# Seven block products for the last layer of the second half of the tokens, and kept weight parts in DRAM

## The chip, the cores and the metric

The kernel runs on one core of one Trainium2 chip. The metric is device microseconds for one execution, as the median of three runs. A core has TensorE (matmuls, written PE in the profile, with its weight loads listed apart as PEld), VectorE (DVE), ScalarE (ACT), GpSimd (POOL) and SyncE (SP), which here only issues transfers. Each engine works through its own instructions in order and waits for other engines by semaphores. Matmul results land in PSUM, which the kernel uses as eight banks of 128 x 512 float32; its GpSimd instructions have all operands in SBUF.

## The reference

```python
x = A_u                                             # 1 x 2048 x 512
h = x + _A_ref(_layernorm(x), ...)                  # a long convolution over the tokens
h2 = h + _B_ref(_layernorm(h), w1, w2, w3, w4)

def _B_ref(x, w1, w2, w3, w4):
    h = _gelu(_layernorm(x) @ w1)                   # layer 1, then a shift of tokens
    hs = shifted(h) @ w2                            # layer 2
    x1 = x + hs
    h2 = _gelu(_layernorm(x1) @ w3) @ w4            # layer 3: 512 -> 1792, layer 4: 1792 -> 512
    return x1 + h2
```

The change is in layers 3 and 4 alone: 2048 tokens, hidden width 1792.

## The kernel before

**Precision.** Each factor of a product is held as a high part (float32r) and a low part (the rest), and a product is three matmuls: high x high, high x low, low x high (`PROD`). A high part is made by ScalarE (a cast, or the GELU written out as float32r), a low part by a subtraction, source minus high part, on VectorE or GpSimd. GELU is therefore done twice on ScalarE: once into the high part, once into a float32 tile from which the low part is taken.

**Layer 3 in seven products.** The loop at the end of `mixer_phase` has 14 steps, `s` = 0 to 13: seven for the first 1024 tokens, seven for the second (`half` is 7). A step makes two hidden blocks of 128, number f and f + 7, for two groups of 512 tokens. That is a 2 x 2 block product and is made from seven block products, a, b, c, e (in `layer3a`) and f, d, g (in `layer3b`), instead of eight: sums and differences of weight blocks (`s1` to `s4`, made by GpSimd in `sum3`) meet sums and differences of activations (`t1` to `t4`). A product is six matmuls (two chunks of 128 of the 512 inputs' halves, three part products) with 512 moving columns into one PSUM bank. VectorE adds the seven banks up (`plus`), ScalarE copies the first. `raw3` loads the weight blocks, `sum3` sums them, `load3` makes their high and low parts on ScalarE and GpSimd. The homes of the parts alternate between odd and even steps.

**Layer 4 before.** The hidden blocks are the stationary operand and the rows of `w4` the moving one: `layer4(s, q, i, ...)` makes 128 tokens of output from the two hidden blocks of the step, six matmuls of 512 columns. A step makes eight such groups, so 48 matmuls, one step after its layer 3: `layer4a(s - 1)` adds four groups up in four PSUM banks that are held over seven steps (`acc`), `layer4b(s - 1)` writes four groups to fresh banks that VectorE adds to `h` in SBUF. At the end of each half `h` gets the last addend and `store` sends it out, four transfers of 64 KB for each 128 tokens; for the second half two of the four are issued by ScalarE's queue. `raw4` and `load4` fetch `w4` and make its parts.

**What sets the order.** `InOrder` keeps the program's order on TensorE, VectorE, ScalarE and GpSimd; transfers are issued by SyncE unless said otherwise. PSUM has four rotating banks (`bank`) and the four that are held (`wide_bank`). A bank is used again when VectorE or ScalarE has read it. VectorE's instructions stand in the order: sums of layer 3 as the products come, low parts of the activations between them, then the additions to `h`.

Of the kernel before, what the change touches and what calls it, by code (L numbers as in the profile page):

```python
# [1150 lines left out]
def mixer_phase(ctx, tc, cst, h, out, finish, w3, w4):  # L1151

    nc = InOrder(tc)
    pool = lambda name, bufs, **kw: ctx.enter_context(tc.tile_pool(name=name, bufs=bufs, **kw))
    sl = pool("slab", 44)
    tm = pool("tm", 6)
    w1a, w1p = pool("wrap0", 1), pool("wrap", 1)
    sm = pool("sm", 2)
    ps = pool("ps2", 4, space=PSUM)
    pa = pool("pacc", 1, space=PSUM)  # L1160
    ident = cst["ident"]
# [2 lines left out]
    def slab(name):  # L1164
        return sl.tile([128, 512], F32R, tag="slab", name=name)

    def slot(i):
        return cst["slab"](i)

    def tmp(name):  # L1170
        return tm.tile([128, 512], F32, tag="g", name=name, bufs=5)

    XQ = [(w1p if i else w1a).tile([128, 4 * 512], F32, name=f"xq{i}") for i in range(4)]
    X1 = {0: XQ[3], 1: XQ[1], 2: XQ[2], 3: XQ[0]}
    quarter = lambda t, i: t[:, i * 512 : i * 512 + 512]
    turned = lambda t: t.rearrange("p (a c x) -> p c a x", a=4, c=4)
# [22 lines left out]
    PROD = ((0, 0), (0, 1), (1, 0))  # L1199
# [47 lines left out]
    def turn1(q):  # L1247
        XT[q] = transposed(XL.pop(q), f"xt{q}", 2 if q == 3 else 0)
# [71 lines left out]
    xq = {}  # L1320
# [79 lines left out]
    def some(n):  # L1400
        while n and todo:
            todo.pop(0)()
            n -= 1


    W3S = [w1p.tile([128, 512], F32R, name=f"w3s{i}") for i in range(2)]
    raw = {n: w1p.tile([128, k * 512], F32, name=f"raw{n}") for n, k in (("a", 1), ("b", 1), ("4", 1), ("5", 1), ("s", 2))}

    def raw3(s):
        f = s % half  # L1410
# [5 lines left out]
    def sum3():  # L1416
# [4 lines left out]
        nc.gpsimd.tensor_tensor(s2, s1, a11, ALU.subtract)  # L1421
        nc.gpsimd.tensor_tensor(s4, a12, s2, ALU.subtract)

    def load3(s, low=nc.gpsimd, parts=range(3)):
        ra, a22, sm_ = raw["a"], raw["b"][:, 256:512], raw["s"]
        if s % 2:
            one, four, last = (slot(11), slot(14)), (slots(4, 2), slots(6, 2)), slot(8)
        else:
            one, four, last = (slot(20), W3S[0]), (slots(16, 2), slots(18, 2)), W3S[1]
        for i, (src, (hi, lo)) in enumerate(((ra, one), (sm_, four), (a22, (last[:, 0:256], last[:, 256:512])))):  # L1430
            if i not in parts:
                continue
            nc.scalar.copy(hi, src)
            low.tensor_tensor(lo, src, hi.bitcast(F32), ALU.subtract)
        at_ = lambda w, i: w[:, i * 256 : i * 256 + 256]
        W3[s] = dict(a11=[at_(w, 0) for w in one], a12=[at_(w, 1) for w in one], a22=[at_(last, i) for i in range(2)],
                     **{f"s{i + 1}": [at_(w, i) for w in four] for i in range(4)})

    def raw4(s):
        for i in range(2):  # L1440
            f = s % half + i * half
# [48 lines left out]
    t1, t3, t2, t4 = ([S[c][i] for c in range(2)] for i in range(4))  # L1490
# [64 lines left out]
    def store(j):  # L1555
        for c in range(4):
            queue = nc.scalar if j >= 8 and c % 2 else nc.sync
            queue.dma_start(ov[c][:, j, :], h[c * 32 : c * 32 + 32, j, :])

    def layer4(s, q, i, b, first, last):  # L1560
        for k in range(2):
            for n, (wi, xi) in enumerate(PROD):
                nc.tensor.matmul(b, H3[s, k, q][xi][:, i * 128 : i * 128 + 128], W4[s][k][wi],
                                 start=(first and k == 0 and n == 0), stop=(last and k == 1 and n == 2))

    def layer4a(s):
        first, last = s % half == 0, s % half == half - 1
        for i in range(4):
            if first:
                acc[i] = wide_bank(i, f"acc{s}_{i}")  # L1570
            layer4(s, 0, i, acc[i], first, last)
            j = s // half * 8 + i
            if last:
                nc.vector.scalar_tensor_tensor(h[:, j, :], h[:, j, :], off1[:, j : j + 1], acc[i], ALU.add, ALU.add)
                store(j)

    def layer4b(s, late):
        for i in range(4):
# [14 lines left out]
            for c in range(2):  # L1593
                halve(FT[1, "sums", c][n], 1, n, c)

    for s in range(2 * half):
        turn, last = s + 1 == half, s + 1 == 2 * half
        layer3a(s)
        if turn:
            fresh(("b11", "t2", "t3", "t1"))  # L1600
        if last:
            load4(s)
        else:
            load3(s + 1, *((nc.gpsimd,) if s else (nc.vector, (2,))))
        if s + 2 < 2 * half:
            raw3(s + 2)
        if s:
            layer4a(s - 1)
        if s == 1:
            for j in range(8, 12):  # L1610
                residual(j), stats2(j)
        if s == 2:
            for j in range(12, 16):
                stats2(j)
            norm2(2)
            for j in range(12, 16):
                residual(j)
# [7 lines left out]
        if not last and s:  # L1625
            load4(s), raw4(s + 1)
        if s + 2 < 2 * half:
            sum3()
        if s:
            layer4b(s - 1, late)  # L1630
        else:
            late()
        some(4)
        if turn:
            fresh(("b21", "t4", "b22"))
    layer4a(2 * half - 1), layer4b(2 * half - 1, lambda: None)


@with_exitstack
# [41 lines left out]
```

## Time and profile before

| | |
|---|---|
| timed runs | 684.05, 684.76, 684.91 us; median 684.76 |
| profiled execution, first to last instruction (its span) | 683.0 us |
| busy over the span: PE, DVE, ACT, POOL | 640.8, 547.9, 415.5, 402.9 us |
| step 0 of the loop starts (first matmul of `l3a`) | 392.1 us |
| step 7 starts (second half) | 524.7 us |
| step 13 starts | 647.1 us |

The page gives no other time of the profiled execution than its span; the median of the runs lies 1.8 us above the span. In the rows of the profile every line is L86, since the wrapper of `InOrder` records each instruction; tiles tell them apart. `l3a` to `l3g` are the banks of layer 3, `acc` the held banks and `l` (or `l4`) the fresh banks of layer 4, `u` the float32 sums of layer 3, `h_...h` and `h_...l` high and low parts of activations. Names such as `cs0w`, `amp0w`, `sn1w` and `ptw` are buffers of the first part of the kernel that now hold weights. A row of the timeline has the start in us, the duration in us, engine, line, operation, output, inputs, shape and count; the bracket behind is the engine's idle time before it and what ended it.

### The profile page before, as it was taken

Reading aid. Unit: us, or ns where it says so; the run is one execution under the profiler, and the core shown is the slowest. Engines: PE = TensorE matmul, PEld = TensorE weight load, DVE = VectorE, ACT = ScalarE, POOL = GpSimd, SP = SyncE. Lnnn points to the kernel's source line nnn. Section 1 sums busy time; section 2 is a strip of 40 time slices with the busy share of each in tenths; the row PEclk is TensorE's granted clock in tenths of the full one; section 3 lists DMA queues with packets and bytes.
Section 4 is the critical chain, followed back from the end, with each engine's and each line's share of the span. In section 5 each row is a group of like instructions: output and inputs, shape, how many; then the busy total and the mean of one; then the engine's idle time right before and its main releaser. Section 6 shows DMA issues by size and latency. Waiting matters only on the chain.

```text
span 683.0 us, 17273 instructions
## 1 busy us (share of the span) xinstructions
PE 640.8 (94%) x7044; PEld 501.2 (73%) x7044; DVE 547.9 (80%) x935; ACT 415.5 (61%) x731; POOL 402.9 (59%) x421
## 2 busy tenths in 40 slices
PE   2985999899999999999999999999999999999997
PEld 2972755673577685768888878888888888888885
DVE  6989989999998999889978798866789954455554
ACT  6998978978889886246634454544375443354330
POOL 1878499878999998402676219355635555554210
PEclk9996999999999999999999999999999999999999
DMA  8840554011301133020232312133312342211004
GB/s 214 241 168 18 157 159 125 2 49 34 65 18 34 34 110 96 2 63 1 63 92 56 100 32 62 32 101 105 103 32 53 87 138 62 63 47 47 24 9 123
DMA packets 49267, 51.52 MB, mean 75 GB/s; under 512 B 6436, under 2 KB 33060, under 8 KB 49188
## 3 DMA queue, kind: packets, MB, share of 16 engines
q1 hardware_dynamic: 47524, 47.80, 24.7%
q10 hardware_dynamic: 1152, 1.57, 1.0%
q0 software_dynamic: 512, 1.05, 0.6%
q8 instruction: 55, 0.90, 0.6%
q14 instruction: 24, 0.20, 0.1%
HBM read 35.72 MB, written 8.39 MB: 65 GB/s over the span
## 4 chain that ended last, share of the span: by engine, by line
PE 67%; ACT 12%; DVE 11%; POOL 5%; issue 3%; DMA 0%; SPq 0%; ACTq 0%; POOLq 0%; DVEq 0%
PE l L86 24%; PE bank L86 12%; PE acc L86 11%; ACT pt L86 7%; DVE cs L86 3%; PE l3e L86 3%; PE l3b L86 3%; PE l3a L86 3%; PE l3g L86 3%; PE l3d L86 3%; PE l3f L86 3%; PE l3c L86 3%; DVE sn L86 2%; POOL pt L86 2%; DVE u L86 1%
## 5 line engine op out<-in xcount | busy, mean ns | idle before, releaser
L86 POOL TENSOR_TENSOR pt<-p,s 128x512 int32<-128x512 int32 x64 | 73.3, 1161 | 8.6 <-DVE sn L86 8.1
L86 ACT ACTIVATE pt<-pt 128x1056 f32<-128x1056 int32 x64 | 69.8, 1091 | 12.5 <-DVE cs L86 6.4
L86 PE MATMUL bank<-at,tbs 128*64 128x128 f32 (+1 forms) x768 | 63.1, 311 | 2.8 <-ACT u L86 0.9
L86 PEld LDWEIGHTS bank<-at,tbs 128*64 128x64 f32 x768 | 44.7, 134 | 19.1 <-ACT at L86 2.1
L86 PE MATMUL bank<-u,ms 64*128 64x128 f32 x736 | 47.5, 278 | 5.7 <-DVE u L86 1.9
L86 PEld LDWEIGHTS bank<-u,ms 64*128 64x128 f32 x736 | 43.1, 188 | 9.7 <-DVE u L86 2.6
L86 POOL TENSOR_TENSOR cs0w<-raw,cs0w 128x512 fp32r<-128x512 f32 x7 | 9.1, 1297 | 58.8 <-ACT cs0w L86 58.8
L86 PE MATMUL bank<-cs 128*32 128x64 f32 x1024 | 33.1, 228 | 11.0 <-ACT kt L86 5.7
L86 DVE TENSOR_TENSOR cs<-pt,amx 128x512 f32<-128x512 f32 x64 | 41.2, 680 | 2.3 <-ACT amx L86 1.7
L86 PEld LDWEIGHTS bank<-cs 128*32 128x32 f32 x1024 | 24.3, 113 | 24.2 <-POOL pt L86 8.4
L86 POOL TENSOR_TENSOR sn1w<-raw,sn1w 128x512 fp32r<-128x512 f32 x7 | 9.5, 1359 | 54.0 <-ACT sn1w L86 42.1
L86 DVE TENSOR_TENSOR h<-h,l 128x512 f32<-128x512 f32 x48 | 32.0, 685 | 10.6 <-PE l L86 10.6
L86 PE MATMUL bank<-ident 128*128 128x128 f32 x292 | 39.6, 293 | 0.0
L86 DVE TENSOR_TENSOR u<-u,l3f 128x512 f32<-128x512 f32 x14 | 9.5, 682 | 36.9 <-PE l3f L86 36.9
L86 ACT COPY at<-bank 128x512 f32<-128x512 f32 x44 | 26.9, 623 | 19.2 <-PE bank L86 19.2
L86 PEld LDWEIGHTS bank<-ident 128*128 128x128 f32 x292 | 36.5, 204 | 2.8 <-DVE at L86 1.1
L86 ACT ACTIVATE pt<-pt,halfpi 128x1056 f32<-128x1056 f32 x32 | 37.8, 1182 | 0.5
L86 ACT ACTIVATE u<-u 128x512 f32<-128x512 f32 x56 | 35.4, 632 | 1.8
L86 POOL TENSOR_TENSOR cs<-pt,amp 128x512 f32<-128x512 f32 x26 | 31.8, 1223 | 5.6 <-ACT pt L86 2.9
L86 DVE STREAM_TRANSPOSE at<-bank 128x512 f32<-128x512 f32 (+1 forms) x36 | 32.8, 950 | 1.4 <-PE bank L86 1.4
L86 PE MATMUL bank<-sn 128*32 128x64 f32 x1024 | 32.5, 225 | 0.0
L86 POOL TENSOR_TENSOR sn<-pt,amp 128x512 f32<-128x512 f32 x24 | 29.5, 1230 | 4.8 <-issue 3.7
(1180 smaller groups left out, 2112.8 us busy)
## 6 DMA issues: line engine op xcount, KB each, us to landing
raw<-in_B_w_dram SPq DMA_DIRECT2D x28, 256.0 KB, 2.7
xq<-xq SPq DMA_DIRECT2D x72, 64.0 KB, 2.0
h<-in_A_u_dram SPq DMA_DIRECT2D x32, 128.0 KB, 4.2
h<-in_A_u_dram SPq DMA_DIRECT2D x16, 256.0 KB, 3.9
rawa<-in_B_w_dram SPq DMA_DIRECT2D x14, 256.0 KB, 2.8
rawb<-in_B_w_dram SPq DMA_DIRECT2D x14, 256.0 KB, 2.9
ms<-in_mm_dram SPq DMA_DIRECT2D x4, 768.0 KB, 10.9
out_dram<-h SPq DMA_DIRECT2D x48, 64.0 KB, 1.7
```

Of the source, the lines that this page charges most:

```text
L86: ins = f(*args, **kw)
```

## The change

Three things change in the loop.

1. **Weight parts of layer 3 are kept.** In the first half each step's seven tiles of high and low parts of `w3` (256 KB each) are written to DRAM (`keep3`, five transfers from SyncE's queue). In the second half `fetch3` reads them back one step ahead, five transfers, in place of `raw3`, `sum3` and `load3`.
2. **Layer 4 of steps 7 to 12 is made from seven products.** The output for 1024 tokens is a 2 x 2 block product as well: two groups of 512 tokens by two halves of 256 output columns, with the two hidden blocks in the middle. `prod4` makes one product: 12 matmuls with 256 moving columns into two banks. VectorE makes sums of activations (`sum4`), ScalarE their high parts (`cast4`), VectorE their low parts (`low4`); GpSimd makes sums and low parts of the `w4` blocks (`load4s`). The products `a11 b11` and `s2 t2` are added up in the four held banks (`res`) over six steps. `v`, `w` and `z` are added to `h` by VectorE (`collect`); `x` and `y`, which two output blocks need, are added up in SBUF (`held`).
3. **Low parts of the second half's hidden blocks are made by GpSimd** instead of VectorE.

In step 13 the parts that were held back are brought into `h`: GpSimd adds `held` (eight additions), ScalarE copies two held banks to `both`, VectorE makes `total`, GpSimd adds both to two output blocks (four additions), `x` and `y` are collected twice each, and VectorE adds `total` to the two other blocks (four additions). Step 13's own layer 4 is done as before, 48 matmuls of 512 columns, behind the loop. Step 7 still does the old layer 4 for step 6.

```diff
+    def homes3(s):
+        if s % 2:
+            return (slot(11), slot(14)), (slots(4, 2), slots(6, 2)), slot(8)
+        return (slot(20), W3S[0]), (slots(16, 2), slots(18, 2)), W3S[1]
...
+    def keep3(s):
+        one, four, last = homes3(s)
+        for far, w in zip(kept[s], (*one, *four, last)):
+            nc.sync.dma_start(far, w.bitcast(F32))
+    def fetch3(s):
+        one, four, last = homes3(s)
+        for far, w in zip(kept[s - half], (*one, *four, last)):
+            nc.sync.dma_start(w.bitcast(F32), far)
+        names3(s)
...
-    for s in range(2 * half):
+    for s in range(half):
...
-        if last:
-            load4(s)
+        if turn:
+            fetch3(s + 1)
         else:
             load3(s + 1, *((nc.gpsimd,) if s else (nc.vector, (2,))))
...
+        if s == 0:
+            keep3(0)
         if turn:
             fresh(("b21", "t4", "b22"))
-    layer4a(2 * half - 1), layer4b(2 * half - 1, lambda: None)
+        else:
+            keep3(s + 1)
...
+    def load4s(s):
+        b1, b2, t = raw["4"], raw["5"], raw["s"]
+        t1, t2, t3, t4 = (part2(t, i) for i in range(4))
+        nc.gpsimd.tensor_tensor(t1, part2(b1, 1), part2(b1, 0), ALU.subtract)
...
+        for src, pair in ((part2(b1, 0), one), (b2, two), (t, four)):
+            nc.scalar.copy(pair[0], src)
+            low_of(pair, src, nc.gpsimd)
...
+    def prod4(s, x, w, banks, more=False, done=True):
+        for n, b in enumerate(banks):
+            for i in (2 * n, 2 * n + 1):
+                for k, (wi, xi) in enumerate(PROD):
+                    nc.tensor.matmul(part2(b, i % 2), OPS[s, x][xi][:, i * 128 : i * 128 + 128], B4[s][w][wi], ...)
...
+    for s in range(half, 2 * half):
+        last, pre = s + 1 == 2 * half, s - 1
+        summed = pre >= half
+        if not last:
+            fetch3(s + 1)
+        if last:
+            for k, c in ((0, (0, 1)), (1, (1, 0)), (0, (1, 1)), (1, (1, 1))):
+                for d, b in zip(columns(*c), held[k]):
+                    nc.gpsimd.tensor_tensor(d, d, b, ALU.add)
+        one = slab(f"one_{s}").bitcast(F32)
+        nc.scalar.copy(one, prod(s, "a", "a11", "b11"))
+        if summed:
+            sum4(pre, "s1", "a21", "a22", ALU.add)
+            sum4(pre, "s2", "s1", "a11", ALU.subtract)
+            sum4(pre, "s3", "a11", "a21", ALU.subtract, SRC[pre, "a21"])
+            for n in ("s2", "s1", "s3"):
+                cast4(pre, n)
+        two, three, four = (tmp(f"{n}_{s}") for n in ("two", "three", "four"))
+        plus(two, prod(s, "b", "s2", "t2"), one)
+        if summed:
+            sum4(pre, "s4", "a12", "s2", ALU.subtract)
+            cast4(pre, "s4")
+            low4(pre, "s2"), low4(pre, "s1")
+        plus(three, prod(s, "c", "s3", "t3"), two)
+        if summed:
+            low4(pre, "s3"), low4(pre, "s4")
+        b = prod(s, "e", "s1", "t1")
+        plus(four, b, three)
+        plus(two, b, two)
+        gelus3(s, "a22", four, four)
+        low4(s, "a22", nc.gpsimd)
+        plus(one, prod(s, "f", "a12", "b21"), one)
+        gelus3(s, "a11", one, one)
+        low4(s, "a11", nc.gpsimd)
+        if summed:
...
+            prod4(pre, "a11", "b11", res[:2], pre > half, last)
+            prod4(pre, "s2", "t2", res[2:], pre > half, last)
+        else:
+            layer4a(pre)
+        (load4 if last else load4s)(s)
+        if not last:
+            raw4(s + 1)
+        if last:
+            both, total = ([slab(f"{n}{i}").bitcast(F32) for i in range(2)] for n in ("both", "total"))
+            for i in range(2):
+                nc.scalar.copy(both[i], res[i])
+            for i in range(2):
+                nc.vector.tensor_tensor(total[i], res[2 + i], both[i], ALU.add)
+            for c, src in (((0, 0), both), ((1, 1), total)):
+                for d, b in zip(columns(*c), src):
+                    nc.gpsimd.tensor_tensor(d, d, two_tiles(b), ALU.add)
+        plus(three, prod(s, "d", "a22", "t4"), three)
+        gelus3(s, "a12", three, three)
+        plus(two, prod(s, "g", "s4", "b22"), two)
+        gelus3(s, "a21", two, two, last)
+        if not last:
+            low4(s, "a12", nc.gpsimd)
+        if not summed:
+            layer4b(pre, lambda: None)
+            continue
+        for n, x, w, c in (("v", "a12", "b21", (0, 0)), ("w", "s4", "b22", (0, 1)), ("z", "a22", "t4", (1, 0))):
+            b = fresh_banks(s, n)
+            prod4(pre, x, w, b)
+            collect(columns(*c), b)
+            if last and n == "w":
+                low4(s, "a12")
+        for k, n, x, w, c in ((0, "x", "s1", "t1", (0, 1)), (1, "y", "s3", "t3", (1, 0))):
+            b = fresh_banks(s, n)
+            prod4(pre, x, w, b)
+            if last:
+                collect(columns(*c), b), collect(columns(1, 1), b)
+            else:
+                collect(held[k], b, pre == half)
+        if last:
+            low4(s, "a21")
+            for c in ((0, 1), (1, 0)):
+                for d, b in zip(columns(*c), total):
+                    nc.vector.tensor_tensor(d, d, two_tiles(b), ALU.add)
...
+        for i in range(4):
+            b = bank(f"l4_{s}_{q}{i}") if q else wide_bank(i, f"acc{s}_{i}")
+            layer4(s, q, i, b, True, True)
+            j = 8 + 4 * q + i
+            nc.vector.scalar_tensor_tensor(h[:, j, :], h[:, j, :], off1[:, j : j + 1], b, ALU.add, ALU.add)
+            store(j)
```

More of the change, by code (lines that the diff above doesn't have):

```diff
@@ L1158, in mixer_phase @@
     sm = pool("sm", 2)
+    w3p = pool("kept", 1, space=bass.MemoryType.DRAM)
     ps = pool("ps2", 4, space=PSUM)
@@ L1171, in tmp @@
         return tm.tile([128, 512], F32, tag="g", name=name, bufs=5)
-    XQ = [(w1p if i else w1a).tile([128, 4 * 512], F32, name=f"xq{i}") for i in range(4)]
+    XQ = [(w1p if i else w1a).tile([128, 4 * 512], F32, tag=f"xq{i}", name=f"xq{i}") for i in range(4)]
     X1 = {0: XQ[3], 1: XQ[1], 2: XQ[2], 3: XQ[0]}
@@ L1406, in mixer_phase @@
     W3S = [w1p.tile([128, 512], F32R, name=f"w3s{i}") for i in range(2)]
-    raw = {n: w1p.tile([128, k * 512], F32, name=f"raw{n}") for n, k in (("a", 1), ("b", 1), ("4", 1), ("5", 1), ("s", 2))}
+    raw = {n: w1p.tile([128, k * 512], F32, tag=f"raw{n}", name=f"raw{n}") for n, k in (("a", 1), ("b", 1), ("4", 1), ("5", 1), ("s", 2))}
     def raw3(s):
@@ L1422, in sum3, with names3 @@
         nc.gpsimd.tensor_tensor(s4, a12, s2, ALU.subtract)
+    def homes3(s):
+        if s % 2:
+            return (slot(11), slot(14)), (slots(4, 2), slots(6, 2)), slot(8)
+        return (slot(20), W3S[0]), (slots(16, 2), slots(18, 2)), W3S[1]
+    def names3(s):
+        one, four, last = homes3(s)
+        at_ = lambda w, i: w[:, i * 256 : i * 256 + 256]
+        W3[s] = dict(a11=[at_(w, 0) for w in one], a12=[at_(w, 1) for w in one], a22=[at_(last, i) for i in range(2)],
+                     **{f"s{i + 1}": [at_(w, i) for w in four] for i in range(4)})
+    kept = {s: [w3p.tile([128, n * 512], F32, name=f"kept{s}{i}") for i, n in enumerate((1, 1, 2, 2, 1))] for s in range(half)}
+    def keep3(s):
[3 more added lines that the diff above has]
+    def fetch3(s):
+        one, four, last = homes3(s)
+        for far, w in zip(kept[s - half], (*one, *four, last)):
+            nc.sync.dma_start(w.bitcast(F32), far)
+        names3(s)
     def load3(s, low=nc.gpsimd, parts=range(3)):
         ra, a22, sm_ = raw["a"], raw["b"][:, 256:512], raw["s"]
[L1426 to L1429, printed above, removed]
+        one, four, last = homes3(s)
         for i, (src, (hi, lo)) in enumerate(((ra, one), (sm_, four), (a22, (last[:, 0:256], last[:, 256:512])))):
@@ L1434, in load3 @@
             low.tensor_tensor(lo, src, hi.bitcast(F32), ALU.subtract)
-        at_ = lambda w, i: w[:, i * 256 : i * 256 + 256]
-        W3[s] = dict(a11=[at_(w, 0) for w in one], a12=[at_(w, 1) for w in one], a22=[at_(last, i) for i in range(2)],
-                     **{f"s{i + 1}": [at_(w, i) for w in four] for i in range(4)})
+        names3(s)
     def raw4(s):
@@ L1594, in fresh @@
                 halve(FT[1, "sums", c][n], 1, n, c)
-    for s in range(2 * half):
-        turn, last = s + 1 == half, s + 1 == 2 * half
+    for s in range(half):
+        turn = s + 1 == half
         layer3a(s)
@@ L1600, in mixer_phase @@
             fresh(("b11", "t2", "t3", "t1"))
-        if last:
-            load4(s)
+        if turn:
+            fetch3(s + 1)
         else:
             load3(s + 1, *((nc.gpsimd,) if s else (nc.vector, (2,))))
-        if s + 2 < 2 * half:
+        if s + 2 < half:
             raw3(s + 2)
@@ L1624, in mixer_phase @@
         late = layer3b(s)
-        if not last and s:
+        if s:
             load4(s), raw4(s + 1)
-        if s + 2 < 2 * half:
+        if s + 2 < half:
             sum3()
@@ L1633, in mixer_phase @@
         some(4)
+        if s == 0:
+            keep3(0)
         if turn:
             fresh(("b21", "t4", "b22"))
-    layer4a(2 * half - 1), layer4b(2 * half - 1, lambda: None)
+        else:
+            keep3(s + 1)
+    XH = [(w1p if i else w1a).tile([128, 4 * 512], F32R, tag=f"xq{i}", name=f"xh{i}") for i in range(4)]
+    spare = w1p.tile([128, 512], F32R, tag="rawa", name="spare")
+    side = lambda i, k: (quarter(XH[i // 2], i % 2 * 2 + k))
+    SUM = {n: (side(i, 0), side(i, 1)) for i, n in enumerate(("s1", "s2", "s3", "s4"))}
@@ new lines, in mixer_phase, with low_of @@
+    part2 = lambda w, i: w[:, i * 256 : i * 256 + 256]
+    pairs = lambda i: XH[2].bitcast(F32).rearrange("p (n t d) -> p n t d", n=4, d=256)[:, i]
+    held = [[pairs(i), pairs(2 + i)] for i in range(2)]
+    OPS, B4, SRC = {}, {}, {}
+    def low_of(pair, src, eng=nc.vector):
+        eng.tensor_tensor(pair[1], src, pair[0].bitcast(F32), ALU.subtract)
+    def load4s(s):
+        b1, b2, t = raw["4"], raw["5"], raw["s"]
+        t1, t2, t3, t4 = (part2(t, i) for i in range(4))
+        nc.gpsimd.tensor_tensor(t1, part2(b1, 1), part2(b1, 0), ALU.subtract)
+        nc.gpsimd.tensor_tensor(t3, part2(b2, 1), part2(b1, 1), ALU.subtract)
+        nc.gpsimd.tensor_tensor(t2, part2(b2, 1), t1, ALU.subtract)
+        nc.gpsimd.tensor_tensor(t4, part2(b2, 0), t2, ALU.subtract)
+        if s % 2:
+            four, two, one = (slots(9, 2), slots(12, 2)), (quarter(XH[3], 3), slot(15)), spare
+        else:
+            four, two, one = (slots(0, 2), XH[3][:, 0:1024]), (slot(2), slot(3)), quarter(XH[3], 2)
+        one = part2(one, 0), part2(one, 1)
+        for src, pair in ((part2(b1, 0), one), (b2, two), (t, four)):
+            nc.scalar.copy(pair[0], src)
+            low_of(pair, src, nc.gpsimd)
+        B4[s] = dict(b11=one, b21=[part2(w, 0) for w in two], b22=[part2(w, 1) for w in two],
+                     **{f"t{i + 1}": [part2(w, i) for w in four] for i in range(4)})
@@ new lines, in prod4, with columns @@
+    def prod4(s, x, w, banks, more=False, done=True):
+        for n, b in enumerate(banks):
+            for i in (2 * n, 2 * n + 1):
+                for k, (wi, xi) in enumerate(PROD):
+                    nc.tensor.matmul(part2(b, i % 2), OPS[s, x][xi][:, i * 128 : i * 128 + 128], B4[s][w][wi],
+                                     start=(i % 2 == 0 and k == 0 and not more), stop=(i % 2 == 1 and k == 2 and done))
+    def columns(q, c):
+        return [h[:, 8 + 4 * q + 2 * n : 10 + 4 * q + 2 * n, c * 256 : c * 256 + 256] for n in range(2)]
@@ new lines, in mixer_phase, with collect, gelus3 @@
+    two_tiles = lambda b: b.rearrange("p (t d) -> p t d", t=2)
+    def collect(dst, banks, new=False):
+        for d, b in zip(dst, banks):
+            if new:
+                nc.vector.tensor_copy(d, two_tiles(b))
+            else:
+                nc.vector.tensor_tensor(d, two_tiles(b), d, ALU.add)
+    def gelus3(s, name, src, dst, high=True):
+        if high:
+            OPS[s, name] = slab(f"h_{name}{s}h"), slab(f"h_{name}{s}l")
+            nc.scalar.activation(OPS[s, name][0], src, AF.Gelu_apprx_tanh)
+        nc.scalar.activation(dst, src, AF.Gelu_apprx_tanh)
+        SRC[s, name] = dst
@@ new lines, in sum4 @@
+    def sum4(s, name, a, b, op, dst=None):
+        t = slab(f"{name}_{s}f").bitcast(F32) if dst is None else dst
+        nc.vector.tensor_tensor(t, SRC[s, a], SRC[s, b], op)
+        SRC[s, name], OPS[s, name] = t, SUM[name]
+    cast4 = lambda s, name: nc.scalar.copy(OPS[s, name][0], SRC[s, name])
+    low4 = lambda s, name, eng=nc.vector: low_of(OPS[s, name], SRC[s, name], eng)
+    fresh_banks = lambda s, name: [bank(f"l4{name}{n}_{s}") for n in range(2)]
+    res = None
+    for s in range(half, 2 * half):
[33 more added lines that the diff above has]
+        if summed:
+            if pre == half:
+                res = [wide_bank(i, f"res{i}") for i in range(4)]
+            prod4(pre, "a11", "b11", res[:2], pre > half, last)
+            prod4(pre, "s2", "t2", res[2:], pre > half, last)
+        else:
+            layer4a(pre)
[31 more added lines that the diff above has]
+                collect(columns(*c), b), collect(columns(1, 1), b)
+            else:
+                collect(held[k], b, pre == half)
[4 more added lines that the diff above has]
+                    nc.vector.tensor_tensor(d, d, two_tiles(b), ALU.add)
@@ L1639, in tile_kernel @@
+    s = 2 * half - 1
+    for q in range(2):
+        for k in range(2):
+            H3[s, k, q] = OPS[s, ("a11", "a12", "a21", "a22")[2 * q + k]]
+        for i in range(4):
[4 more added lines that the diff above has]
+            store(j)
 @with_exitstack
```

## The prediction

> **What bounds the kernel now.** I read the page first, then busy time by stage, then the chain of waits.
>
> ```profile
> span 683.0 us, 17273 instructions
> PE 640.8 (94%) x7044; PEld 501.2 (73%) x7044; DVE 547.9 (80%) x935; ACT 415.5 (61%) x731; POOL 402.9 (59%) x421
> ```
> ```profile
> core 0: us, PE busy (x) PEld busy (x) DVE busy (x) ACT busy (x) POOL busy (x), PEclk, DMA share, GB/s
> 606.30:626.70 20.40, 20.40 (x91) 16.90 (x90) 10.08 (x15) 8.55 (x14) 9.70 (x10) 1.00 0.17 52
> 647.13:683.00 35.87, 31.44 (x139) 25.72 (x137) 16.52 (x24) 6.79 (x11) 2.54 (x2) 0.99 0.27 72
> ```
> ```profile
> 626.89 1.36 PE l3a L86 x6
> ...
> 647.29 1.36 PE l3a L86 x6
> ...
> 673.13 5.45 PE l L86 x24
> ```
>
> TensorE is busy 94% of the span. The stage row 606.30:626.70 is one whole step of the second half (step 11): 20.40 us, TensorE busy in all of it at full clock, VectorE for 10.08, ScalarE 8.55, GpSimd 9.70. The chain holds matmuls alone, one step every 20.40 us (647.29 less 626.89), to the end at 678.58. So what leaves other engines in a step is worth nothing; only shorter TensorE work is, as long as no other engine takes the bound. Step 13 and what follows it last 35.87 us; I call that stage the tail.
>
> **Part one, the matmuls.**
>
> ```profile
> 569.84 0.39 PE L86 MATMUL l3e<-t110l,cs1w 128*128 128x512 f32 x1
> 570.06 0.39 PE L86 MATMUL l3e<-t110h,sn0w 128*128 128x512 f32 x1
> ...
> 258.61 1.61 PE L86 MATMUL bank<-ident 128*128 128x128 f32 x13
> ...
> 291.55 1.88 PE L86 MATMUL bank<-h,ident 128*128 128x512 f32 x4
> ```
> ```profile
> 258.62 1.42 PEld L86 LDWEIGHTS bank<-ident 128*128 128x128 f32 x12
> ```
> ```profile
> L86 PEld LDWEIGHTS acc<-cs0w,h_000h x8: 187/188/188, 407.1 to 412.0; 128*128 128x128 f32 x8
> ```
> ```profile
> L86 PE MATMUL bank<-ident x292: 275/275/422, 14.6 to 291.4; 128*128 128x128 f32 x146
> ...
> L86 PE MATMUL bank<-h,ident x20: 592/592/697, 156.3 to 295.8; 128*128 128x512 f32 x20
> ```
>
> A product of six matmuls takes 1.36, so a matmul of 512 columns comes every 0.2267 us. A step now has 42 for layer 3 (9.52) and 48 for layer 4 (10.88). In steps 8 to 13 the 48 become 7 x 12 = 84 matmuls of 256 columns, each with a weight load of its own. No row shows a float32r matmul of 256 columns. Bounds: the 13 `ident` matmuls, each with a load of 128 columns, take 1.61 us, the last of them 0.275 of it: (1.61 - 0.275) / 12 = 0.111 from one to the next, load included, and I take that as the least. From above: the recorded load, 0.188, if none of it is hidden. Between them lies half of 0.2267, 0.113, if all the time goes with the columns. I take 0.120: of the plain float32 kind, 128 columns cost 0.111 and 512 cost (1.88 - 0.59) / 3 = 0.43, so 0.00083 a column and 0.005 beside them; a float32r matmul of 512 in 0.2267 must run at about half that per column, 0.21, which leaves 0.0135 to 0.016 that don't go with the columns, and 256 then take 0.120 to 0.121. So 84 x 0.120 = 10.08, a gain of 0.80 a step; at 0.111 it is 1.56, at 0.188 a loss of 4.91. Five steps (8 to 12) earn 4.0 (7.8; -24.6); step 13 is treated below. Step 7 stays at 20.40.
>
> [...]
>
> **Part two, VectorE and GpSimd in steps 8 to 12.**
>
> ```profile
> 443.22 1.88 DVE L86 TENSOR_TENSOR h<-h,l 128x512 f32<-128x512 f32 x3
> 434.48 2.49 DVE L86 TENSOR_TENSOR h<-h,xq 128x512 f32<-128x512 f32 x4
> 532.62 1.78 DVE L86 TENSOR_TENSOR b2211l<-xq,b2211h 128x512 fp32r<-128x512 f32 x1
> ```
> ```profile
> 532.11 1.75 POOL L86 TENSOR_TENSOR w3s<-rawa,ptw 128x512 fp32r<-128x512 f32 x1
> 583.30 1.29 POOL L86 TENSOR_TENSOR sn1w<-raw,sn1w 128x512 fp32r<-128x512 f32 x1 [10.62 <-ACT sn1w L86]
> 589.96 2.41 POOL L86 TENSOR_TENSOR sn0w<-raws,cs1w 128x1024 fp32r<-128x1024 f32 x1
> 592.32 0.75 POOL L86 TENSOR_TENSOR sn0w<-rawb,sn0w 128x256 fp32r<-128x256 f32 x1
> ```
>
> VectorE's additions of 512 elements follow each other every 0.60 us (three in 1.88, four in 2.49, less the 0.69 of the last). A step has 7 `plus`, 4 sums, 4 low parts and 10 collects: 25 x 0.605 = 15.1 of 19.6. TensorE fills a bank of the last five products every 0.72, VectorE empties one in 0.605; with four banks that lies behind the matmuls. If VectorE took 0.69 each it would still fit (17.3). GpSimd: four sums and a low part of 256 (5 x 0.70), one of 512 and three of activations (4 x 1.25), one of 1024 (2.37): 10.9; it starts when ScalarE has the first GELU, some 9 us into the step, and ends about 1 us into the next. ScalarE: 7 GELUs, 4 casts, 3 weight casts and a copy, about 9.3. All three are under 19.6: cost 0. Taking the four low parts from VectorE is worth 0, since TensorE's busy time already fills the step.
>
> One thing has a price. The last row of VectorE and the first of GpSimd overlap: both instructions have two SBUF operands, and both last about 1.75, where alone they last 0.69 and 1.29. They go in turns: 1.25 for GpSimd's, 0.5 for the other. VectorE's eight instructions of this kind stand at the start of a step; in steps 8 to 12 GpSimd is then nearly idle.
>
> **Part three, the kept weights.**
>
> ```profile
> far<-xs SPq DMA_DIRECT2D x8, 256.0 KB, 3.0
> ```
> ```profile
> 486.70 1.77 DVE L86 TENSOR_TENSOR xq<-xq,xq 128x512 f32<-128x512 f32 x1 [1.97 <-DMA raw<-in_B_w_dram]
> ```
>
> Seven tiles of 256 KB a step, written in the first half and read in the second; one like it lands in 3.0 us, so seven in turn need at most 21 and overlapped far less, with the engines' share at 0.17 of a step. A fetch is issued a step ahead; it waits in SP's queue until the products of the step before have read its homes, and behind it stand only `raw4`'s loads, needed a step later. A write waits for GpSimd's low parts, and the next step's `raw3` stands behind it. The only place where a later landing would hurt is 486.70, where VectorE waits for the swap of `xq`, whose transfers stand in SP's queue. In the program's order `keep3(4)` stands a step before that swap, `keep3(5)` behind it. Bounds 0 and +5 (one step's writes, some 7 us if three are under way at once, less some 2 us that TensorE had in spare banks there; estimates); I take 0, since the order keeps them apart. The removed `load3` and `sum3` of the second half free GpSimd and ScalarE: 0.
>
> **Part four, step 13.** Here the order changes: ahead of everything GpSimd gets eight additions of `held`, VectorE gets 12 more instructions, and the last eight additions to `h` with their 32 store transfers stand behind all of them.
>
> ```profile
> 599.09 0.63 ACT L86 ACTIVATE h_1000h<-u 128x512 fp32r<-128x512 f32 x1 [5.50 <-DVE u L86]
> 599.76 0.63 ACT L86 ACTIVATE u<-u 128x512 f32<-128x512 f32 x1
> ...
> 603.02 1.12 ACT L86 CAST cs0w<-raw 128x512 fp32r<-128x512 f32 x2
> 607.89 0.59 ACT L86 COPY u<-l3a 128x512 f32<-128x512 f32 x1 [3.75 <-PE l3a L86]
> ```
> ```profile
> 669.09 0.75 DVE L86 SCALAR_TENSOR_TENSOR h<-h,rn,acc 128x512 f32<-128x512 f32 x1 [0.67 <-PE acc L86]
> ...
> 678.61 0.69 DVE L86 TENSOR_TENSOR h<-h,l 128x512 f32<-128x512 f32 x1 [0.67 <-PE l L86]
> ```
> ```profile
> L86 ACTq DMA_DIRECT2D out_dram<-h x16: 373/418/443, 669.9 to 679.7; - x16
> ```
>
> From the first matmul of step 13: VectorE is free at 0.85. Up to the sum of product f stand 5 `plus` (3.0) and the eight SBUF instructions. GpSimd's eight additions of 512 run at once, so they go in turns: of the eight I put one at 0.6, two at 1.15 (behind a `plus`, during which GpSimd goes on) and five at 1.75, together 11.65. f is summed at 15.5, the sum before the GELUs at 14.3. ScalarE then does four GELUs (0.67 each), two casts (1.1) and the first `both` (0.6): 18.8. Until then VectorE waits; then two `total`, d and g: 21.2. Meanwhile the banks of d and g stop TensorE. GpSimd: 0.85 + 8 x 1.75 = 14.8, low part after the second GELU at 17.0, three more by 20.8, two additions of `both` by 23.3. The first output block is collected only then: 23.9. Then w, a low part (1.2), z, x, y: 12 x 0.605 + 1.2 makes 32.4; low part and four `total` additions 35.4; the first of the eight last additions 36.2. Each queue issues two transfers of 0.42 for a group: eight groups 6.7, so 42.9, against one group every 1.36 before. From the last issue (679.7 + 0.43 = 680.2) to the end of the span were 2.8: the tail is 45.7 instead of 35.87, a loss of 9.8. Bounds: without turns, every SBUF instruction at 0.6, the same walk puts the first last addition at 29.9 and the tail at about 40.1, +4.2 (the 48 matmuls then end last); with all eight at 1.75 it is 2.3 worse, +12.1.
>
> Sum: 683.0 - 4.0 + 9.8 = 688.8 for the span. The median of the runs shown lies 1.8 above this execution's span, which I leave as it is: 690.5, slower.
>
> **The rivals.** *TensorE's 48 last matmuls hide step 13 (faster).* They take 10.9 us in which VectorE has time to catch up. For it: 37 x 0.605 + 8 x 0.75 is 28.4 of VectorE work, under the 32.2 us in which it was done before (679.3 less 647.1). Against it: VectorE stands still while ScalarE's queue and GpSimd's come to `both`. It decides where the first of the eight last additions starts: 36.2 - 0.75 = 35.4 in my walk; from 29.6 on (35.87 + 4.0 less 2.8, 6.7 and 0.75) the change loses. If it is hidden whole, six steps earn 0.80: 678.2, time 680.0.
>
> *The turns cost nothing (no change).* GpSimd's additions write and read strided columns of `h`, which no row shows against VectorE; if they let it pass, +4.2 - 4.0: 685.0. Row 532.62 speaks against.
>
> *The loads come out.* If each short matmul waits for its recorded load, steps take 9.52 + 84 x 0.188 = 25.3: +24.6 + 9.8, 719. Against it: 12 loads in 1.42. [...]
>
> *The kept weights come late.* +5 on top: 695.5.
>
> **How the numbers follow.** Likeliest, TensorE faster by 4 to 8 and the tail worse by 7 to 12: 0.60, its own range 686.5 to 694. Turns cost nothing: 0.14. Hidden tail: 0.16. Late transfers: 0.05. Loads: 0.05. A difference of 0.2% (1.4 us) is about what can be told from no change. Faster 0.17 (the hidden tail and a little of the second), same 0.14, slower 0.69. The range 682.5 to 696 leaves out the loads and most of the hidden tail.
>
> **What would show it.** Six short matmuls in 0.72 us; steps 8 to 12 at 19.6 each, TensorE busy throughout; in step 13 GpSimd additions to `h` of about 1.75 and VectorE sums beside them as long, TensorE idle for 7 us or more at w and z, eight last additions back to back after the last matmul or near it, stores without pauses, a tail near 46. I am wrong if the short matmuls come at 0.15 or more, if TensorE stalls in steps 8 to 12, or if the tail is under 40.

## The result and the profile after

| kernel | median (lowest to highest, runs) |
|---|---|
| before | 684.84 us (684.05 to 684.97, 4) |
| after | 692.51 us (692.03 to 693.13, 4) |

The changed kernel is slower: ratio 1.0113, 95% interval 1.0098 to 1.0127, 7.7 us by the medians. Its profiled execution has a span of 690.2 us, 7.2 over the 683.0 of before.

The page of the changed kernel, its busy times and the clock in 40 slices:

```profile
span 690.2 us, 17910 instructions
...
PE 640.5 (93%) x7260; PEld 511.7 (74%) x7260; DVE 587.3 (85%) x1003; ACT 416.8 (60%) x736; POOL 419.4 (61%) x434
...
PEclk9996999999999999999999999999999999999978
```

TensorE has 216 matmuls more and is busy for as long as before (640.8), VectorE and GpSimd are busy for 39.4 and 16.5 us longer. The two last slices of the clock, a 7 and an 8, were both 9 before. The 8 belongs to the 6.8 us behind the last matmul (1.00 from 672.9 up to 683.4, 0.73 from there to the end, by busy time in these two stretches); the 7 is new, and the last section comes back to it. Where the time went is read by stage. Step 12 and the tail (step 13 and all behind it) of the changed kernel, with busy times, granted clock, DMA share and GB/s:

```profile
core 0: us, PE busy (x) PEld busy (x) DVE busy (x) ACT busy (x) POOL busy (x), PEclk, DMA share, GB/s
623.28:642.92 19.64, 19.64 (x128) 17.96 (x127) 16.28 (x26) 8.86 (x15) 10.97 (x11) 1.00 0.14 41
642.92:690.20 47.28, 34.58 (x176) 29.85 (x174) 36.62 (x47) 9.81 (x17) 23.82 (x17) 0.85 0.15 45
```

A step takes 19.64 instead of 20.40 with TensorE busy in all of it: the five steps bring 3.8 to 3.9. Step 13 starts at 642.92, 4.2 earlier than before (647.13; the rest of the 4.2 stands ahead of step 7, which starts 0.3 to 0.4 earlier). The tail lasts 47.28 instead of 35.87: 11.4 lost. 11.4 less 4.2 is the 7.2 of the span.

Inside the tail, VectorE's rows of the timeline (start, duration, what, number of instructions, and in brackets the idle time before the first and what ended it):

```profile
643.73 1.73 DVE L86 TENSOR_TENSOR s_12f<-two,four 128x512 f32<-128x512 f32 x1
645.50 1.66 DVE L86 TENSOR_TENSOR s_12f<-s_12f,one 128x512 f32<-128x512 f32 x1
...
658.48 0.68 DVE L86 TENSOR_TENSOR one<-one,l3f 128x512 f32<-128x512 f32 x1
662.02 1.29 DVE L86 TENSOR_TENSOR total<-res,both 128x512 f32<-128x512 f32 x2 [2.87 <-ACT both L86]
...
665.61 0.69 DVE L86 TENSOR_TENSOR h<-l4v,h 128x512 f32<-128x512 f32 x1 [1.10 <-POOL h L86]
666.85 0.69 DVE L86 TENSOR_TENSOR h<-l4v,h 128x512 f32<-128x512 f32 x1 [0.55 <-POOL h L86]
...
678.75 2.71 DVE L86 SCALAR_TENSOR_TENSOR h<-h,rn,acc 128x512 f32<-128x512 f32 x4
681.39 2.73 DVE L86 SCALAR_TENSOR_TENSOR h<-h,rn,l 128x512 f32<-128x512 f32 x4
```

GpSimd's and ScalarE's rows beside them (ACTq is ScalarE's DMA queue):

```profile
643.62 13.20 POOL L86 TENSOR_TENSOR h<-h,xh 128x512 f32<-128x512 f32 x8
659.37 1.28 POOL L86 TENSOR_TENSOR h_a2213l<-four,h_a2213h 128x512 fp32r<-128x512 f32 x1 [2.55 <-ACT four L86]
...
664.28 2.53 POOL L86 TENSOR_TENSOR h<-h,both 128x512 f32<-128x512 f32 x2
```
```profile
661.42 1.06 ACT L86 COPY both<-res 128x512 f32<-128x512 f32 x2
...
679.52 7.87 ACTq L86 DMA_DIRECT2D out_dram<-h  x16
```

Read from the top: while GpSimd adds `held` to `h` (eight instructions in 13.20, 1.65 each), VectorE's eight instructions that read two SBUF operands last 1.2 to 1.8 instead of 0.69. The sum of f comes out at 659.2, 16.2 after the start of step 13. Then VectorE waits for ScalarE (2.87, `both`), then for GpSimd (1.10 and 0.55), and from 666.85 it runs without a gap to 684.1. The first of the eight last additions starts 35.8 after the start of step 13, and the 16 transfers of ScalarE's queue last 7.87 without a pause (7.63 on SyncE's). GpSimd is done with `held` at 656.8 and then waits 2.55 for ScalarE (the row at 659.37), so its additions don't hold up what stands behind them in its own queue; they act through VectorE. In the tail of before, VectorE waited for TensorE at each of the last eight additions; here it is the chain of VectorE and GpSimd that ends last.

### The profile page after: what moved, and what is told of

It is laid out like the page before. It is cut to its first block, busy times and chain, and to the rows that moved or that the text cites. A ratio compares the mean times of both kernels' runs of the same rounds, so it can differ in the third digit from the quotient of the medians.

```text
span 690.2 us, 17910 instructions
## 1 busy us (share of the span) xinstructions
PE 640.5 (93%) x7260; PEld 511.7 (74%) x7260; DVE 587.3 (85%) x1003; ACT 416.8 (60%) x736; POOL 419.4 (61%) x434
## 4 chain that ended last, share of the span: by engine, by line
PE 59%; ACT 12%; DVE 12%; POOL 8%; issue 4%; DMA 2%; SPq 1%; POOLq 0%; ACTq 0%; DVEq 0%
PE l L86 18%; PE bank L86 11%; ACT pt L86 7%; PE acc L86 6%; DVE cs L86 3%; PE l3d L86 3%; PE l3a L86 3%; PE l3g L86 3%; PE l3e L86 3%; PE l3c L86 3%; PE l3b L86 3%; PE l3f L86 3%; DVE h L86 2%; PE res L86 2%; POOL h L86 2%
## 5 line engine op out<-in xcount | busy, mean ns | idle before, releaser
L86 PEld LDWEIGHTS bank<-at,tbs 128*64 128x64 f32 x768 | 44.7, 134 | 19.1 <-ACT at L86 2.1
L86 DVE TENSOR_TENSOR u<-xs,bank 128x1024 f32<-128x1024 f32 x23 | 28.1, 1221 | 3.9 <-ACT xs L86 2.6
L86 DVE TENSOR_TENSOR amx<-E,amx 128x512 f32<-128x512 f32 (+1 forms) x32 | 25.4, 793 | 4.9 <-ACT amx L86 4.8
L86 POOL TENSOR_TENSOR amp<-E,ec 128x512 f32<-128x512 f32 x23 | 25.2, 1103 | 4.1 <-DVE ec L86 3.6
L86 POOL TENSOR_TENSOR cs0w<-raw,cs0w 128x512 fp32r<-128x512 f32 x4 | 5.2, 1298 | 36.5 <-ACT cs0w L86 36.5
L86 ACT ACTIVATE xq<-xq,qo,qr 128x512 f32<-128x512 f32 x15 | 11.0, 806 | 24.7 <-DVE qo L86 24.7
```

The lines of the kernel that those rows point to most:

```text
L86: ins = f(*args, **kw)
```

## The experiments

My theory: the loss is VectorE's, held up by GpSimd's reading in turns with it, and then by the queues of ScalarE and GpSimd ahead of the first output block. Rivals: GpSimd's busy time alone, VectorE's number of instructions, TensorE's lower clock, the kept weights or the low parts. The runs of the kernel before beside these gave 685.21 us (684.27 to 685.86, 13 runs) for the first four and 685.03 us (683.42 to 685.82, 15 runs) for the last two.

### Without the additions of the held parts

The parts of x and y that were held over steps 7 to 11 are missing from this kernel's output.

```diff
-        if last:
-            for k, c in ((0, (0, 1)), (1, (1, 0)), (0, (1, 1)), (1, (1, 1))):
-                for d, b in zip(columns(*c), held[k]):
-                    nc.gpsimd.tensor_tensor(d, d, b, ALU.add)
```

> The changed kernel without GpSimd's eight additions of held in step 13; the sums of x and y over steps 7 to 11 are left out of the output, and all other work stays. Theory (turns and queues in step 13): VectorE's eight SBUF-only instructions take 0.6 each in place of 1.2 to 1.8, f is summed at about 9 us after the step's start instead of 16.2, the first of the eight last additions starts at about 29 instead of 35.8, and the kernel takes 685.5 (684.5 to 686.5). Rival (VectorE's count: 12 more instructions and eight last additions set the end, whoever shares the step): within 1 us of 692.5. Rival (TensorE's half clock between 659.3 and 669.5 is what costs): 10.2 us at half clock are 5.1 lost, so about 687.4, and the stretch of VectorE's work would be shorter only behind the matmuls.

Measured: 685.57 us, one run; span 683.5. VectorE in step 13, which starts at 643.03 here:

```profile
643.84 0.68 DVE L86 TENSOR_TENSOR s_12f<-two,four 128x512 f32<-128x512 f32 x1
644.56 0.69 DVE L86 TENSOR_TENSOR s_12f<-s_12f,one 128x512 f32<-128x512 f32 x1
...
651.49 0.68 DVE L86 TENSOR_TENSOR one<-one,l3f 128x512 f32<-128x512 f32 x1
655.04 1.29 DVE L86 TENSOR_TENSOR total<-res,both 128x512 f32<-128x512 f32 x2 [2.88 <-ACT both L86]
...
658.72 0.69 DVE L86 TENSOR_TENSOR h<-l4v,h 128x512 f32<-128x512 f32 x1 [1.20 <-POOL h L86]
659.95 0.69 DVE L86 TENSOR_TENSOR h<-l4v,h 128x512 f32<-128x512 f32 x1 [0.54 <-POOL h L86]
...
671.87 2.71 DVE L86 SCALAR_TENSOR_TENSOR h<-h,rn,acc 128x512 f32<-128x512 f32 x4
```

The sums last 0.68, f is summed at 652.2, and the first last addition starts 28.8 after the start of step 13. 6.9 us of the result are these eight instructions, though they stand on an engine that is not the bound. The tail that remains is 683.5 - 643.0 = 40.5, still 4.6 over that of before, which eats the 4 us of the steps. In it VectorE still waits 2.88 for ScalarE's `both` and 1.20 and 0.54 for GpSimd's `h`.

TensorE's clock is another difference between the two kernels: it falls to half in the changed kernel (last section) and stays at 1.00 in this one:

```profile
652.00:658.50 6.50, 6.50 (x44) 5.83 (x42) 2.65 (x5) 4.97 (x10) 6.12 (x5) 1.00 0.00 0
658.50:668.00 9.50, 8.02 (x52) 6.91 (x51) 8.74 (x14) 0.91 (x2) 3.91 (x4) 1.00 0.01 2
```

It does not explain the 6.9 us. Up to the sum of f, 7.1 are lost (16.2 against 9.1), and in the changed kernel that sum is done at 659.16, just before the clock falls at 659.26. From the first `total` to the first last addition both kernels take the same, 16.73 with the fall (662.02 to 678.75) and 16.83 without (655.04 to 671.87).

### The same time on GpSimd, without reading

```diff
-            for k, c in ((0, (0, 1)), (1, (1, 0)), (0, (1, 1)), (1, (1, 1))):
-                for d, b in zip(columns(*c), held[k]):
-                    nc.gpsimd.tensor_tensor(d, d, b, ALU.add)
+            for k in range(8):
+                nc.gpsimd.memset(XH[2].bitcast(F32)[:, k % 2 * 1024 : k % 2 * 1024 + 1024], 0.0)
```

> The eight additions of held are replaced by eight memsets of 1024 columns on GpSimd, which read no SBUF; the same part of the output is left out as without the additions. It keeps GpSimd busy at the start of step 13 and takes the shared reading away. Theory (VectorE and GpSimd go in turns because both read two SBUF operands): VectorE's eight instructions take 0.6 to 0.7 each though GpSimd works beside them, f at about 9, and the time is that of the kernel without the additions plus at most what GpSimd's later low parts cost, 685 to 687.5. Rival (GpSimd's busy time as such slows VectorE, or its queue alone makes the loss): VectorE's instructions stay at 1.2 to 1.8 or the first last addition stays at 34 or later, 690 or more.

Measured: 685.53 us, one run; span 683.4. GpSimd, then VectorE, of that kernel:

```profile
643.56 7.25 POOL L86 MEMSET xh<- 128x1024 f32 x8
```
```profile
643.69 0.68 DVE L86 TENSOR_TENSOR s_12f<-two,four 128x512 f32<-128x512 f32 x1
644.40 0.69 DVE L86 TENSOR_TENSOR s_12f<-s_12f,one 128x512 f32<-128x512 f32 x1
...
651.33 0.68 DVE L86 TENSOR_TENSOR one<-one,l3f 128x512 f32<-128x512 f32 x1
```

GpSimd is busy with writes alone for 7.25 us, over the same VectorE sums, and none of them is longer. So it isn't GpSimd being busy, nor its writing to SBUF, that holds VectorE up here; what the additions have and the memsets lack is the reading of two SBUF operands. (The memsets take 7.25, the additions 13.20; that half of the cover was not tried. The additions also read and write strided columns of `h`, the memsets write a tile without gaps; no run separates the two, but in the kernel before the row at 532.62 of the prediction shows VectorE and GpSimd just as slow beside each other, 1.78 and 1.75, without such columns.) VectorE's first sum takes 1.73 beside the additions and 0.68 beside the memsets.

### Another way without held parts: x and y collected twice in every step

```diff
-        if last:
-            for k, c in ((0, (0, 1)), (1, (1, 0)), (0, (1, 1)), (1, (1, 1))):
-                for d, b in zip(columns(*c), held[k]):
-                    nc.gpsimd.tensor_tensor(d, d, b, ALU.add)
...
-            if last:
-                collect(columns(*c), b), collect(columns(1, 1), b)
-            else:
-                collect(held[k], b, pre == half)
+            collect(columns(*c), b), collect(columns(1, 1), b)
```

> x and y are added to both of their output blocks by VectorE in every step, so held and GpSimd's eight additions are gone and nothing is left out. VectorE then has 29 instructions a step instead of 25. Theory: 29 x 0.605 = 17.5 still lies behind TensorE's 19.6, steps 8 to 12 stay at 19.6 to 19.7, VectorE comes about 2 us later into step 13, f is summed at about 11 and the first last addition starts at about 31: 687.8 (686.5 to 689). Rival (VectorE becomes the bound of every step, at 0.69 an instruction): steps of 20.0 or more, 690 or more. Rival (count): no better than 692.

Measured: 688.03 us (687.72 to 688.20, 4 runs), ratio 1.0042, interval 1.0027 to 1.0057. The whole computation is made. Step 12 and the tail:

```profile
624.20:644.07 19.87, 19.87 (x128) 18.02 (x127) 18.38 (x30) 8.86 (x15) 10.97 (x11) 1.00 0.08 28
644.07:686.20 42.13, 31.77 (x175) 27.07 (x174) 31.19 (x50) 9.71 (x17) 12.24 (x10) 0.97 0.19 55
```

Four more collections bring VectorE to 18.38 of 19.87 in a step. The step lengthens by 0.23, 1.1 over five steps; why by just that I did not follow. VectorE begins step 13 later, so the tail is 1.7 longer than without the additions (42.13 against 40.47), and 5.2 shorter than with them. More VectorE instructions and a shorter time: its count alone doesn't explain the result.

### The kept weights alone

The kernel before with `homes3`, `keep3` and `fetch3` of the change, and the calls that belong to them; `raw3` and `sum3` end with the first half:

```diff
         if last:
             load4(s)
+        elif s + 1 >= half:
+            fetch3(s + 1)
         else:
             load3(s + 1,
...
+        if s == 0:
+            keep3(0)
...
+        elif s + 1 < half:
+            keep3(s + 1)
```

> The kernel before with the kept weight parts alone: five writes a step in the first half, fetches in place of the loads, sums and splits of the second half, old layer 4, low parts on VectorE. Theory: TensorE is busy throughout either way, 684.8 (684.3 to 685.3), steps at 20.4. Rival (the writes delay the swap of xq or the fetches come late): TensorE waits in steps 4 to 7, 686.5 or more. Rival (GpSimd and ScalarE freed help): under 684.

Measured: 684.55 us (683.48 to 685.66, 10 runs), ratio 0.9996, interval 0.9986 to 1.0005: nothing. The place that I had named as the only one where a later landing would hurt, VectorE's first swap of `xq`, in this run and then in the changed kernel:

```profile
488.22 1.36 DVE L86 TENSOR_TENSOR xq<-xq,xq 128x512 f32<-128x512 f32 x1 [4.73 <-DMA xq<-xq]
```
```profile
483.75 0.69 DVE L86 TENSOR_TENSOR h<-h,l 128x512 f32<-128x512 f32 x1 [0.67 <-PE l L86]
488.69 1.83 DVE L86 TENSOR_TENSOR xq<-xq,xq 128x512 f32<-128x512 f32 x1 [4.26 <-DMA xq<-xq]
```

It did come later, by 1.5 and 2.0 us (486.70 before). Step 7 starts at 523.40 and 524.35 all the same (524.7 before), so this lay in the slack.

### The low parts on GpSimd alone

```diff
-        return lambda: nc.vector.tensor_tensor(lo, src, hi.bitcast(F32), ALU.subtract)
+        return lambda: (nc.gpsimd if s >= half else nc.vector).tensor_tensor(lo, src, hi.bitcast(F32), ALU.subtract)
```

> One part of the change alone, in the kernel before: the low parts that follow the GELUs of the third layer in steps 7 to 13 are made by GpSimd instead of VectorE, in the same places of the order; nothing else differs. My theory (an edit off the path that sets the end costs nothing): GpSimd is idle for about half of those steps and the fourth layer reads the low parts last, so 684.8 to 685.4. Rival (the later low parts stop TensorE): GpSimd takes 1.30 us for 512 columns where VectorE takes about 0.7, four of them a step stand behind each other, and if TensorE waits 1 us for them in each of seven steps it is 690 to 692. Second rival (VectorE relieved of four instructions a step shortens the tail): about 683.

Measured: 685.22 us (684.27 to 685.83, 10 runs), ratio 1.0005, interval 0.9995 to 1.0014: nothing. Step 11 by its busy times, and the first matmuls of steps 12 and 13:

```profile
606.30:626.70 20.40, 20.40 (x92) 16.89 (x91) 7.47 (x12) 8.55 (x14) 14.80 (x14) 1.00 0.19 50
```
```profile
626.21 0.39 PE L86 MATMUL l3a<-b1110h,ptw 128*128 128x512 f32 x1
...
646.61 0.39 PE L86 MATMUL l3a<-b1110h,sn1w 128*128 128x512 f32 x1
```

VectorE has 7.47 instead of 10.08 in a step, GpSimd 14.80 instead of 9.70, TensorE 20.40 of 20.40 as before.

### Another order of step 13

On top of the kernel with the double collection: `both` is copied as soon as product g is issued, w and z come ahead of v, the additions of `total` go to GpSimd, the parts of `w4` (`load4`) stand behind its additions of `both`, and the collections into the last block stand behind the third of the last eight additions.

```diff
+            for i in range(2):
+                nc.scalar.copy(both[i], res[i])
         gelus3(s, "a21", two, two, last)
...
+            for d, b in zip(columns(0, 0), both):
+                nc.gpsimd.tensor_tensor(d, d, two_tiles(b), ALU.add)
+            load4(s)
...
+            collect(columns(0, 1), product("w", "s4", "b22"))
+            for i in range(2):
+                nc.vector.tensor_tensor(total[i], res[2 + i], both[i], ALU.add)
+            collect(columns(1, 0), product("z", "a22", "t4"))
+            low4(s, "a12")
+            collect(columns(0, 0), product("v", "a12", "b21"))
+            x_ = product("x", "s1", "t1")
+            collect(columns(0, 1), x_)
+            y_ = product("y", "s3", "t3")
+            collect(columns(1, 0), y_)
+            low4(s, "a21")
+            for c in ((0, 1), (1, 1), (1, 0)):
+                for d, b in zip(columns(*c), total):
+                    nc.gpsimd.tensor_tensor(d, d, two_tiles(b), ALU.add)
...
             store(j)
+            if (q, i) == (0, 2):
+                collect(columns(1, 1), x_), collect(columns(1, 1), y_)
```

> The kernel of collect_twice with the order of step 13 changed and all of the output made: ScalarE makes both copies directly behind product g, the fourth layer begins with products w and z (their blocks need no addition of `both` first), v, x and y follow, the collections of x and y into the last block stand behind the third of the last eight additions, and the eight additions of `total` are GpSimd's, behind its two of `both`. My theory (the tail is VectorE's chain from the sum of f to the last addition; the steps cost 19.87 as in collect_twice): step 13 starts at 644.1 as there, and the tail falls from 42.1 to about 37, so a span of 681 and 682 to 684.5 in all: level with the kernel before or a little under it. Rival (the moved additions share GpSimd's turns with VectorE again, 8 x 1.3 us of them, and what GpSimd takes from VectorE comes back): the tail stays at 40 to 42 and the time at 686 to 688. Rival (the relation of VectorE's count to the steps sets all): no change from 688.0.

(The additions of `total` are six, not eight.) Measured: 682.55 us (682.47 to 683.02, 5 runs), ratio 0.9966, interval 0.9953 to 0.9978: 2.5 us under the kernel before and 10.0 under the changed one. Its tail, and VectorE and GpSimd in it:

```profile
644.14:680.70 36.56, 31.29 (x175) 26.83 (x174) 29.97 (x46) 9.62 (x17) 18.31 (x14) 0.97 0.23 65
```
```profile
654.34 0.68 DVE L86 TENSOR_TENSOR one<-one,l3f 128x512 f32<-128x512 f32 x1
655.50 0.69 DVE L86 TENSOR_TENSOR three<-three,l3d 128x512 f32<-128x512 f32 x1 [0.48 <-PE l3d L86]
...
665.96 1.46 DVE L86 TENSOR_TENSOR h_a2113l<-two,h_a2113h 128x512 fp32r<-128x512 f32 x1
667.34 1.39 DVE L86 SCALAR_TENSOR_TENSOR h<-h,rn,acc 128x512 f32<-128x512 f32 x2
...
674.93 0.75 DVE L86 SCALAR_TENSOR_TENSOR h<-h,rn,l 128x512 f32<-128x512 f32 x1 [0.67 <-PE l L86]
```
```profile
664.32 7.99 POOL L86 TENSOR_TENSOR h<-h,total 128x512 f32<-128x512 f32 x6 [0.74 <-DVE h L86]
```

The waits for `both` and for GpSimd's `h` are gone, and near the end VectorE waits for TensorE again (0.67): the tail is 36.56, 0.7 over that of before, while step 13 starts 3.0 earlier. Several things were moved at once, so what each of them brings is not shown. GpSimd's six additions of `total` read two SBUF operands here as well; they stand where VectorE mostly collects from PSUM, and of VectorE's rows only the low part at 665.96 (1.46) shows them. So the seven products gain in this kernel once step 13 isn't ordered against them.

## Why the prediction was right, and where it was off

Forecast 690.5, measured 692.51, slower for the reason given. Of the 2.0 us between them, 1.6 are the tail, and 0.5 come from the runs' median lying 2.3 above the span here instead of 1.8; the start of step 13, 4.2 instead of 4.0 earlier, takes 0.2 off. By its steps:

**The matmuls (gain 4.0).** Product y of step 12 and the first matmul of step 13, by TensorE's timeline:

```profile
641.48 0.40 PE L86 MATMUL l4y<-sn1w,xh 128*128 128x256 f32 x2
...
642.92 0.40 PE L86 MATMUL l3a<-b1110h,sn1w 128*128 128x512 f32 x1
```

Twelve in 1.44: 0.120 each, the value taken. The load that belongs to each, 0.19 by its row, is hidden, though loads are busy for 17.96 of the 19.64 of step 12. Gain 3.8 to 3.9.

**The steps' other engines, the low parts, the kept weights (0).** TensorE is busy in all of step 12. For the low parts and the kept weights it is shown by the two runs that do one part alone; both intervals hold 1. VectorE had 16.28 in step 12 (15.1 worked out), GpSimd 10.97 (10.9), ScalarE 8.86 (9.3).

**The tail (loss 9.8; measured 11.4).** That the additions make the loss, and not GpSimd's busy time or its writing, is shown by two runs: without them, and with writing in their place, 7 us go away and the sums are back at 0.68. Each is a single run, but 7 us are about three times the widest spread of the runs of one kernel (2.4). That the two engines go in turns is an estimate from the lengths of the rows (1.73 and 1.65 beside each other); no run shows it by itself. The walk against the trace, from the start of step 13:

| step of the walk | predicted | measured |
|---|---|---|
| f summed | 15.5 | 16.2 |
| first `total` begins | 18.8 | 19.1 |
| first output block collected | 23.9 | 24.6 |
| first of the last eight additions begins | 35.4 | 35.8 |
| from there to the end | 10.3 | 11.45 |
| tail | 45.7 | 47.28 |

The term that was mis-sized is the last but one: I had the stores at 0.84 for a group, two transfers of 0.42 on each queue, which is what they take with pauses between; in a row they took 7.87 / 8 = 0.98; why they take longer in a row, no run shows. That is 1.15 of the 1.6. What VectorE loses beside the additions makes the rest: of VectorE's eight instructions I had put one at 0.6, but each of them is held up (the first lasts 1.73), so f came 0.7 later, of which 0.4 is left at the last additions.

**The rivals.** "The turns cost nothing" gave 685.0 for a kernel without turns; the two runs without them gave 685.5. "The tail is hidden" was to decide at 29.6 after the start of step 13. That point was wrong: without the additions the last eight began at 28.8, and the kernel was no faster. With 7.98 for the stores, as measured there (its queue issues from 672.64 to 680.62), instead of 6.7, the point is 35.87 + 4.0 - 2.8 - 8.0 - 0.75 = 28.3, which agrees. My bound for a tail without turns, 40.1, was 40.5.

**The signs to look for.** Six matmuls in 0.72, steps of 19.6, GpSimd additions at 1.65 beside VectorE sums as long, stores without pauses and a tail near 46 are there. TensorE's stall I had put at w and z and at 7 us or more; it is at v and w (and 0.86 in the second product into the held banks, ahead of a low part):

```profile
652.32 0.39 PE L86 MATMUL res<-cs0w,xh 128*128 128x256 f32 x1 [0.86 <-DVE xh L86]
...
658.62 0.39 PE L86 MATMUL l4v<-cs0w,h_a1212h 128*128 128x256 f32 x1 [1.97 <-DVE two L86]
...
664.05 0.77 PE L86 MATMUL l4w<-cs0w,xh 128*128 128x256 f32 x2 [3.01 <-DVE three L86]
```

5.8 together. Product v waits until VectorE has read the bank of e (into `two`), and w until it has read that of d (into `three`): each one product earlier than I had thought. The last additions began 4.2 ahead of the last matmul, not behind it.

## What to carry to other kernels

Work that is moved to an idle engine is not free when it slows the instructions beside it: here eight additions on GpSimd, off the bound by every busy share, cost 7 us because they stood beside VectorE instructions with two SBUF operands (1.2 to 1.8 instead of 0.69), and six like them lengthened a single VectorE row (1.46 instead of 0.68) where VectorE mostly read from PSUM. Here the last step lost nearly three times what five steps had saved, so where work is held back to the end, the walk through the end of the kernel is worth more care than the steps. The time of an issue on a queue with pauses can be too short for one without them (here 0.42 against 0.49); ask what it takes when it issues in a row.

## What the hardware did that I had not expected

TensorE's clock fell in the tail. Three stretches of the changed kernel by busy time, the last but two numbers being the granted clock:

```profile
652.60:659.26 6.66, 4.69 (x28) 3.85 (x28) 6.56 (x7) 1.23 (x3) 4.22 (x3) 1.00 0.00 0
659.26:669.50 10.24, 7.23 (x34) 6.97 (x34) 5.83 (x9) 5.60 (x11) 9.92 (x8) 0.50 0.00 0
669.50:674.50 5.00, 5.00 (x35) 4.63 (x34) 5.00 (x9) 0.00 (x0) 0.00 (x0) 1.00 0.02 3
```

```profile
666.75 0.41 PE L86 MATMUL l4z<-cs0w,h_a2212h 128*128 128x256 f32 x1
...
669.31 0.49 PE L86 MATMUL l4x<-cs0w,xh 128*128 128x256 f32 x2
```

From 659.26 for 10.24 us it was 0.50, and the twelve matmuls of product z took 2.56 there, 0.213 each instead of 0.120. The fall came 0.6 us after a stall of 1.97 (the row at 658.62 above), when TensorE was at work again. No VectorE row of that stretch waits for TensorE: it waited for `both` and for GpSimd's `h`, and from 666.85 it has no gap, so the clock cost nothing that the trace shows, and the kernel without the additions, at full clock, took as long from the first `total` to the first last addition (16.83 against 16.73). That kernel has neither the fall nor the stalls at v and w; one with these stalls and without the fall was not tried. In the kernel that collects twice, a stall of 1.67, ahead of w, left the clock at 1.00:

```profile
659.84 0.48 PE L86 MATMUL l4w<-cs0w,xh 128*128 128x256 f32 x2 [1.67 <-DVE three L86]
```
```profile
659.50:669.00 9.50, 7.71 (x53) 6.96 (x54) 7.79 (x13) 2.41 (x4) 5.64 (x5) 1.00 0.01 3
```

No idle time of TensorE in step 13 before the fall was longer than that 1.97, and the 3.01 ahead of w lies within the 10.24 at 0.50. What lowers the clock there, and what brings it back to 1.00 at 669.50, no run shows.

GpSimd's writing alone did not hold VectorE up (0.68 beside 7.25 us of memsets), and VectorE and GpSimd did not share evenly in the additions: GpSimd's rose from 1.29 to 1.65, VectorE's from 0.69 to between 1.18 and 1.78.
